# An FFT convolution whose last two tiles go through DRAM in more parts

## The chip, the cores and the metric

One core of one Trainium2 chip. The metric is device time in microseconds of one execution of the program; before the change it is 274.76 us, the median of three runs (272.75 to 276.08). Engines are named as in the profile: PE (TensorE matmuls), PEld (its weight loads), DVE (VectorE), ACT (ScalarE), POOL (GpSimd), SP (SyncE, which here only issues DMAs). ACTq and SPq are the DMA-issuing instructions of ACT and SP.

## The reference

```python
H = W = 224; C = 96; K = 7                      # x: (1, H, W, C) bf16, w: (K, K, C, C) bf16
wp = jnp.pad(w, ((0, H - K), (0, W - K), (0, 0), (0, 0)))
Xf = rfft2(x.astype(float32), axes=(1, 2))
Wf = rfft2(wp.astype(float32), axes=(0, 1))
Yf = einsum('bhwi,hwio->bhwo', Xf, Wf)
y = irfft2(Yf, s=(H, W), axes=(1, 2)).astype(bfloat16)
```

So y is the circular 7x7 convolution of a 224x224 image with 96 input and 96 output channels.

## The kernel before

The kernel computes the convolution in another way: a short Fourier transform along the height, the taps along the width. The height is cut into 8 blocks (j) of 28 output rows. Each block, with 6 rows of overlap, is transformed into 17 planes (s, real and imaginary part in r); for each plane the seven taps along the width are a chain of small matmuls over channels. The width is cut into 7 tiles (t = 0 to 6) of 32 pixels, handled as two phases of 16 positions (w). `TL` is the last tile, 6; the change speaks of tile 5 as the sixth.

Three kinds of work run for each tile:

- **A jobs** transform a tile's pixels. The pixels are loaded into two buffers, `xn_bufs` (118 partitions, 3072 elements, one for each half of the blocks), and PE writes the transform by way of PSUM into one of two `xf` buffers. Tile t+1's A jobs run in half-rounds 0 to 26 of tile t.
- **Rounds** (`b_round`): 17 a tile, one a plane. A plane is 33 matmuls of 96 columns (22 in the first and the last plane, `REAL`), with two PSUM banks, one scaling on ACT (tt_), two combining steps on DVE (u, v) and one sum (yf) on POOL or DVE. `yf` collects up to three planes (`YGRP`), then one DMA writes them to a scratch tensor in DRAM, `scr`, laid out [w][j][s][r, channel]. For the last tile these stores are issued by ACT, one round later (`puts`), and the very last one by SP.
- **C jobs** transform back. Planes come from DRAM with (j, s, r) on the partitions: three blocks make 102 rows. `load_t` loads them in five pieces a tile (`LT`: blocks 0-2 and 3-5, each in two halves of 8 positions, and blocks 6-7 in a special layout `tt2`) into `tt` tiles, which `pump` requests as buffers come free. The first request for tile t-1 is made by SP in round 3 of tile t (`queue_c`). A C job multiplies by the matrix `G` (102 x 84), two matmuls of 384 columns, casts from PSUM into a `yo` buffer (four of them, of which two are parts of a J buffer) and, each second job, stores to the output.

The order on each engine is the program's order. A round has two places for other work, `mid` (between its two banks) and `end`, called half-rounds k = 2s and 2s+1; `pace` spreads a list of jobs evenly from half-round a to b. `CQ` says how many C jobs of the two tiles before run in a tile: in tile 6, three of tile 4, then eleven of tile 5, the last of them due before half-round `k1` = 28.

The last tile's planes have no later tile beside which they could be transformed back. Its scratch is in three tensors, planes 0-8 (`scra`), 9-14 and 15-16 (`scrb`). The first is loaded by SP in round 11 into the free `xf` buffer (`tl_a`, 72 partitions for each half of the blocks); the others after the last round, by ACT (two DMAs) and SP (`tl_b`, 128 partitions). The matrices `GA` and `GB` (block-diagonal copies of parts of G, built by `g_parts` with small DMAs in tiles 3 and 4) hold four blocks at once. The last inverse is 16 chunks of 384 columns: `first` multiplies tl_a by GA into a PSUM bank, `second` adds tl_b times GB, `tail_evac` casts to bf16, alternating DVE and ACT. Eight `first` fill the eight PSUM banks; then `WARM` = 36 matmuls on a tile of zeros (`wu`) run; then come the 16 `second`. After each four chunks SP stores 336 KB to the output.

All instructions are recorded by a helper, so the profile gives line 87 for nearly everything; tiles tell them apart.

Of the kernel before, what the change touches and what calls it, by code (L numbers as in the profile page):

```python
# [8 lines left out]
BF16 = mybir.dt.bfloat16  # L9
# [5 lines left out]
B = 28  # L15
# [5 lines left out]
NJ = 8  # L21
# [12 lines left out]
YGRP = ((0, 3), (3, 6), (6, 9), (9, 12), (12, 15), (15, 17))  # L34
YGRPL = ((0, 3), (3, 6), (6, 9), (9, 12), (12, 15), (15, 17))
SA = 9
SB = 15
YMAX = 3
YBUF = 4
JGB = ((0, 3), (3, 6), (6, 9), (9, 12), (12, 15), (15, 17))  # L40
# [2 lines left out]
SH2 = (0, 8, 13, 17)  # L43
MERGE = ()
NP2 = 0
WARM = 36
BIAS = 3000.0


# [5 lines left out]
def kernel(  # L55
# [76 lines left out]
    def dma(out_ap, in_ap):  # L132
        return DE.dma_start(out=out_ap, in_=in_ap)
# [9 lines left out]
    KB = (NJ * 2 * (SB - SA), NJ * 2 * (NS - SB))  # L143
    assert sum(KB) == 128
    XW = 2 * TW * C
    xn_bufs = [cpool.tile([R, XW + 32], BF16, name=f"xn{i}") for i in range(2)]

# [341 lines left out]
    def b_round(t, s, mid, end, ydve=False, planes=()):  # L489
# [5 lines left out]
            1: (Jb[:, 6], Jb[:, 3], Jb[:, 2]),  # L495
            2: (Jb[:, 5], Jb[:, 1], Jb[:, 0]),
        }
        for (y0, y1) in (YGRPL if t == TL else YGRP):
# [77 lines left out]
            end()  # L576
        if s == y1 - 1:
            dst, yo0 = scr_tiles[t], 0
            if t == TL:
                i = (s >= SA) + (s >= SB)  # L580
                dst, yo0 = scr_tiles[(t, i)], (0, SA, SB)[i]
# [25 lines left out]

    TW2 = 2 * TW * C
    tl_all = xf_bufs[(TL + 1) % 2].rearrange("c p r s w j -> c (p r s w j)")
    tl_a = [tl_all[0:KA, g * TW2:(g + 1) * TW2].rearrange("p (w e) -> p w e", e=2 * C) for g in range(2)]  # L610
    tl_b = tl_all[:, 2 * TW2:3 * TW2].rearrange("p (w e) -> p w e", e=2 * C)

    def load_b(i, eng, nh):
        sb = scr_tiles[(TL, 1 + i)].rearrange("w j s (r e) -> (j s r) w e", r=2)
        for h in range(nh):
            w0, w1 = h * TW // nh, (h + 1) * TW // nh
            eng.dma_start(out=tl_b[i * KB[0]:i * KB[0] + KB[i], w0:w1], in_=sb[:, w0:w1])

    def g_parts():
        for j in range(4):  # L620
            dma(GA[j * 2 * SA:(j + 1) * 2 * SA, j * B:(j + 1) * B], G[0:2 * SA, 0:B])
            yield
        for j in range(NJ):
            for i, (s, s1) in enumerate(((SA, SB), (SB, NS))):
                n = 2 * (s1 - s)
                dma(GB[i * KB[0] + j * n:i * KB[0] + (j + 1) * n, j // 4, j % 4 * B:(j % 4 + 1) * B], G[2 * s:2 * s1, 0:B])
                yield

    yo_free = [J_bufs[2][0:4 * B, i * PXC * C:(i + 1) * PXC * C] for i in range(2)]
# [8 lines left out]
    def c_jobs(t):  # L638
        jobs = []
        w0 = t * 2 * TW  # L640
        for gi, h in LT:
            hold = {}
            nq = 2 if gi < 2 else 3

            def mk_(q, gi=gi, h=h, nq=nq, hold=hold):
                def put(j0, nj, px, npx, row, col):
                    dma(out[0, j0 * B:(j0 + nj) * B, w0 + px:w0 + px + npx, :].rearrange("h w c -> h (w c)"),
                        hold["yo"][row:row + nj * B, col:col + npx * C])

                def f():  # L650
                    if q % 2 == 0:
                        hold["yo"] = new_yo()
                    tt = tt_tiles[(t, gi, h)]
                    yo = hold["yo"]
                    nj = 2 if q == 2 else 3
                    for b in range(2):
                        pb = bank()[0:nj * B, 0:4 * C]
                        TE.matmul(pb, lhsT=G[0:nj * FR, 0:nj * B],
                                  rhs=tt[0:nj * FR, 4 * q + 2 * b:4 * q + 2 * b + 2, :].rearrange("p w e -> p (w e)"), start=True, stop=True)
# [10 lines left out]
                    if q == nq - 1:  # L670
# [79 lines left out]
    for r in range(NS + LAG):  # L750
# [18 lines left out]
        if r == PGRP[-2][1] + 1:  # L769
            assert not any(q[2] for q in qs[:len(PGRP) - 1])  # L770
            wtmp_cm.__exit__(None, None, None)
            t_pool = ctx.enter_context(tc.tile_pool(name="tt", bufs=NTT, side="right"))
            t2_pool = ctx.enter_context(tc.tile_pool(name="tt2", bufs=1, side="right"))
            yo_pool = ctx.enter_context(tc.tile_pool(name="yo", bufs=2, side="right"))
            g_pool = ctx.enter_context(tc.tile_pool(name="gp", bufs=1, side="right"))
            GA = g_pool.tile([KA, 4 * B], BF16, name="GA")
            GB = g_pool.tile([128, 2, 4 * B], BF16, name="GB")
            GE.memset(GA[:], 0.0)
            GE.memset(GB[:], 0.0)
        if r == NS + 3:  # L780
# [15 lines left out]
    cj = c_jobs(0)  # L796
    gp = g_parts()
    for t in range(2, NT):
        if t == TL:
            scr_tiles[t] = None  # L800
            scr_tiles[(t, 0)] = dr_pool.tile([TW, NJ, SA, 4 * C], BF16, name="scra")
            for i in range(2):
                scr_tiles[(t, 1 + i)] = dr_pool.tile([TW, NJ, (SB - SA, NS - SB)[i], 4 * C], BF16, name=f"scrb{i}")
# [40 lines left out]
    M4 = 4 * B  # L844

    def first(g, q):
        pc = bank()[0:M4, 0:4 * C]
        TE.matmul(pc, lhsT=GA[:], rhs=tl_a[g][:, 2 * q:2 * q + 2, :].rearrange("p w e -> p (w e)"), start=True, stop=False)
        return pc

    def second(g, q, pc, yo):
        TE.matmul(pc, lhsT=GB[:, g], rhs=tl_b[:, 2 * q:2 * q + 2, :].rearrange("p w e -> p (w e)"), start=False, stop=True)
        tail_evac(yo[0:M4, q % 4 * 4 * C:(q % 4 + 1) * 4 * C], pc, 4 * C)
    order = [(g, q) for h in range(2) for g in range(2) for q in range(4 * h, 4 * h + 4)]
    live = {k: first(*k) for k in order[:8]}
    for _ in range(WARM):
        TE.matmul(live[order[7]].rearrange("p (a b) -> p a b", a=3), lhsT=wu[:, 0:M4], rhs=wu[:].unsqueeze(1).to_broadcast([128, 3, 128]),
                  start=False, stop=False)
    LF = 4
    for i, (g, q) in enumerate(order):  # L860
        if q % 4 == 0:
# [40 lines left out]
```

## Time and profile before

| what | value |
|---|---|
| median of three runs | 274.76 us (272.75 to 276.08) |
| span of the profiled execution | 273.5 us |
| PE busy | 259.0 us (95%), 5149 matmuls |
| DVE, ACT, POOL busy | 213.0, 197.2, 94.8 us |
| DMA | 46.78 MB, mean 171 GB/s |
| PE matmul pb<-tt,Gm (C jobs) | 132, mean 326 ns |
| stores scr<-yf | 30 of 288 KB, 6 of 192 KB |
| loads tt<-scr | 24 of 336 KB, 6 of 288 KB, small ones |
| loads xf<-scra / xf<-scrb | 2 of 384 and 2 of 48 KB / 2 of 288 and 1 of 192 KB |

The profile is of one execution. Matmuls overlap, so their mean duration is longer than their spacing. A timeline line merges neighbouring instructions of a kind: start, duration, engine, operation, output<-input, count, and in brackets the idle time before it with what ended it. The chain of waits is followed back from the last instruction. The share called DMA is the mean busy share of the 16 DMA engines. DMA issues show when SP or ACT issued, not when data landed.

### The profile page before, as it was taken

The numbers are of one execution on the slowest core, as the hardware profiler recorded it, in microseconds if no ns is written. First come the engines' busy times: TensorE is split into PE (matmuls) and PEld (weight loads), VectorE is DVE, ScalarE is ACT, GpSimd is POOL, SyncE is SP. The second block draws the span as 40 slices with busy tenths as digits, with TensorE's granted clock in tenths as the row PEclk, the third lists the DMA queues.
The fourth block names the chain that finished last, engine by engine and source line by source line (L and its number), as shares of the span: only waits on it lengthen the run. The fifth ranks groups of instructions, "written<-read, shape, count | busy, mean of one in ns | idle before, by whom it ended". The sixth has DMA issues, their size and how long they took to land.

```text
span 273.5 us, 12147 instructions
## 1 busy us (share of the span) xinstructions
PE 259.0 (95%) x5149; PEld 237.7 (87%) x5149; DVE 213.0 (78%) x455; ACT 197.2 (72%) x485; POOL 94.8 (35%) x156
## 2 busy tenths in 40 slices
PE   8989998999999999999999999999999999899882
PEld 3659898999999989999999989999999999789661
DVE  5629799898979889779787887787977998788232
ACT  5529997668785657988988889888988865666022
POOL 7780032336446523431422222224144314224000
PEclk9999999999999999999999999999999999999999
DMA  6956110641112398996968487889678644797765
GB/s 177 222 119 169 52 47 2 168 135 48 46 47 88 105 288 149 274 263 166 310 172 248 116 228 217 200 205 313 253 194 181 204 162 132 154 297 195 196 120 180
DMA packets 46038, 46.78 MB, mean 171 GB/s; under 512 B 35150, under 2 KB 36954, under 8 KB 45886
## 3 DMA queue, kind: packets, MB, share of 16 engines
q1 hardware_dynamic: 43696, 43.94, 58.9%
q10 hardware_dynamic: 2288, 2.06, 2.7%
q8 instruction: 40, 0.66, 1.1%
q14 instruction: 14, 0.11, 0.1%
HBM read 24.65 MB, written 21.33 MB: 168 GB/s over the span
## 4 chain that ended last, share of the span: by engine, by line
PE 72%; DMA 11%; DVE 7%; ACT 5%; issue 2%; SPq 1%; POOL 1%; DVEq 0%; ACTq 0%
PE pb L87 72%; DMA wq<-in_w_dram 5%; ACT WF L87 3%; DVE WF L87 2%; DVE J L87 2%; DMA xf<-scrb 2%; DMA tt<-scr 2%; DMA scrb<-yf 1%; SPq L87 1%; DVE u L87 1%; DMA scr<-yf 1%; DVE v L87 1%; ACT xf L87 1%; DVE yf L87 1%; POOL yf L87 1%
## 5 line engine op out<-in xcount | busy, mean ns | idle before, releaser
L87 PE MATMUL pb<-WF,J 96*128 96x96 bf16 x2821 | 163.1, 206 | 1.1 <-DVE J L87 0.6
L87 PEld LDWEIGHTS <-J 96*128 96x128 bf16 x2821 | 138.2, 98 | 9.8 <-DVE u L87 1.5
L87 POOL TENSOR_TENSOR yf<-v,u 128x384 bf16<-128x384 f32 x79 | 77.8, 999 | 151.3 <-issue 88.0
L87 ACT CAST xf<-pb 96x408 bf16<-96x408 f32 (+3 forms) x143 | 67.3, 488 | 8.1 <-PE pb L87 6.3
L87 PE MATMUL pb<-WF,xf 96*128 96x96 bf16 x952 | 60.3, 206 | 1.1 <-ACT xf L87 0.5
L87 DVE TENSOR_TENSOR J<-xf 96x1824 bf16<-96x1824 bf16 (+1 forms) x84 | 57.6, 725 | 0.1
L87 PEld LDWEIGHTS <-xf 96*128 96x128 bf16 x952 | 47.3, 98 | 1.8 <-issue 0.9
L87 PE MATMUL pb<-Fm,xn 118*128 118x136 bf16 (+3 forms) x640 | 45.5, 199 | 0.9 <-DVE u L87 0.8
L87 ACT CAST WF<-pb 96x480 bf16<-96x480 f32 (+1 forms) x59 | 29.1, 573 | 6.8 <-PE pb L87 6.8
L87 PE MATMUL pb<-tt,Gm 102*84 102x384 bf16 (+1 forms) x132 | 32.4, 326 | 1.3 <-DMA tt<-scr 1.3
L87 ACT CAST J<-pb 84x384 bf16<-84x384 f32 (+1 forms) x65 | 28.0, 484 | 6.0 <-PE pb L87 3.0
L87 ACT CAST yo<-pb 84x384 bf16<-84x384 f32 (+1 forms) x66 | 28.2, 484 | 5.1 <-PE pb L87 5.1
L87 PEld LDWEIGHTS <-xn 118*128 118x128 bf16 x640 | 30.5, 97 | 1.2 <-issue 1.1
L87 DVE TENSOR_TENSOR J<-J 96x912 bf16<-96x912 bf16 (+2 forms) x42 | 22.8, 542 | 0.0
L87 PE MATMUL pb<-wq 98*128 98x120 bf16 (+1 forms) x288 | 21.3, 226 | 1.0 <-DMA wq<-in_w_dram 1.0
L87 PEld LDWEIGHTS <-wq 98*128 98x128 bf16 x288 | 19.4, 150 | 1.4 <-issue 1.4
L87 PE MATMUL pb<-wu 128*128 128x512 bf16 (+1 forms) x80 | 18.3, 392 | 1.0 <-DVE ct L87 1.0
L87 PEld LDWEIGHTS <-wu 128*128 128x128 bf16 (+1 forms) x80 | 9.4, 120 | 8.8 <-issue 3.3
L87 DVE TENSOR_TENSOR yf<-v,u 128x384 bf16<-128x384 f32 x26 | 14.7, 566 | 0.9
L87 DVE CAST WF<-pb 96x480 bf16<-96x480 f32 (+1 forms) x13 | 7.5, 610 | 6.8 <-PE pb L87 6.7
L87 PEld LDWEIGHTS <-Gm 102*84 102x84 bf16 (+1 forms) x132 | 11.0, 117 | 2.0 <-DMA tt<-scr 1.4
L87 ACT CAST tt<-pb 112x384 bf16<-112x384 f32 x8 | 3.6, 479 | 11.1 <-PE pb L87 11.0
(385 smaller groups left out, 239.7 us busy)
## 6 DMA issues: line engine op xcount, KB each, us to landing
scr<-yf SPq DMA_DIRECT2D x30, 288.0 KB
xn<-in_x_dram SPq DMA_DIRECT2D x12, 672.0 KB
tt<-scr SPq DMA_DIRECT2D x24, 336.0 KB
out_dram<-yo SPq DMA_DIRECT2D x12, 252.0 KB
out_dram<-J SPq DMA_DIRECT2D x12, 252.0 KB
tt<-scr SPq DMA_DIRECT2D x6, 288.0 KB
wq<-in_w_dram SPq DMA_DIRECT2D x1, 1719.0 KB
WF<-in_x_dram SPq DMA_DIRECT2D x2, 672.0 KB
```

What stands on the lines that cost most here:

```text
L87: r = fn(*a, **k)
```

## The change

Four things change; the arithmetic does not.

1. Tile 5's scratch is two tensors, planes 0-7 and 8-16 (`PART5`), with store groups that fit (`YGRP5`). Its blocks 0-5 go, whole rows of 16 positions at once, into the two pixel buffers: the first part in round 14 of tile 5, the second in round 3 of tile 6. Rows there are ordered (part, j, s, r), so a reordered copy of G, `G5`, is built. Blocks 6-7 still go into one `tt2` tile, first part requested in round 1 of tile 6, second in round 3.
2. Tile 6's scratch is five tensors (`LPART`). Their loads are issued by SP in rounds 8, 11 and 14 (`LOADS`); the fourth part is loaded by ACT and the fifth by SP after the last round. `g_parts` makes the matching smaller copies of G.
3. In tile 6 the C jobs end before half-round 24 instead of 28 (`k1`).
4. The last inverse runs in 12 chunks of 512 columns; its output is stored after two and after three chunks of each group of three (8 stores). `WARM` is 22.

```diff
-SB = 15
+LPART = ((0, 6), (6, 9), (9, 12), (12, 15), (15, 17))
+LROW = (0, 48, 0, 48, 96)
+LOADS = (8, 11, 14)
+SP5 = 8
+YGRP5 = ((0, 3), (3, 6), (6, 8), (8, 11), (11, 14), (14, 17))
...
-WARM = 36
+WARM = 22
...
+    def load_l(i, eng):
+        s0, s1 = LPART[i]
+        sv = scr_tiles[(TL, i)].rearrange("w j s (r e) -> (j s r) w e", r=2)
+        halves = [(tl_a[g], g, 2) for g in range(2)] if s0 < SA else [(tl_b, 0, 1)]
+        n = NJ * 2 * (s1 - s0) // len(halves)
+        for buf, g, _ in halves:
+            eng.dma_start(out=buf[LROW[i]:LROW[i] + n].rearrange("p (w e) -> p w e", w=TW), in_=sv[g * n:(g + 1) * n])
+
+    PART5 = ((0, SP5), (SP5, NS))
+
+    def load_5(i, gis):
+        s0, s1 = PART5[i]
+        n = 2 * (s1 - s0)
+        sv = scr_tiles[(TL - 1, i)].rearrange("w j s (r e) -> (j s r) w e", r=2)
+        for gi in gis:
+            if gi < 2:
+                m = -(-3 * n // 16) * 16
+                r0 = i * 6 * SP5
+                dma(xn_bufs[gi][r0:r0 + m, 0:XW].rearrange("p (w e) -> p w e", w=TW), sv[gi * 3 * n:gi * 3 * n + m])
+                continue
+            if i == 0:
+                tt_tiles[(TL - 1, 2, 0)] = t2_pool.tile([128, 12, 2 * C], BF16, name="tt2")
+            tt = tt_tiles[(TL - 1, 2, 0)]
+            for j in range(2):
+                a, b = 2 * s0 + j * FR, (6 + j) * n
+                dma(tt[a:a + n], sv[b:b + n, 0:12])
+                a = 2 * s0 + 2 * FR
+                dma(tt[a:a + n, 4 * j:4 * j + 4], sv[b:b + n, 12:16])
...
-        k1 = 2 * NS if t < TL else 2 * NS - 6
+        k1 = 2 * NS if t < TL else 2 * NS - 10
...
-            if s == 3:
+            if s == 3 and t < TL:
                 queue_c(t - 1)
-            if t in (3, 4):
+            if t == TL - 1 and s == 14:
+                load_5(0, (0, 1))
+            if t == TL and s == 1:
+                load_5(0, (2,))
+            if t == TL and s == 3:
+                load_5(1, (0, 1, 2))
+            if t in (3, 4, 5):
                 next(gp, None)
-            if t == TL and s == SA + 2:
-                sv = scr_tiles[(TL, 0)].rearrange("w j s (r e) -> (j s r) w e", r=2)
-                for g in range(2):
-                    for p0, p1 in ((0, 64), (64, KA)):
-                        dma(tl_a[g][p0:p1], sv[g * KA + p0:g * KA + p1])
+            if t == TL and s in LOADS:
+                load_l(LOADS.index(s), DE)
...
-    load_b(0, SE, 2)
-    load_b(1, DE, 1)
+    load_l(3, SE)
+    load_l(4, DE)
...
-        if q % 4 == 3:
-            w0 = TL * 2 * TW + q // 4 * PXC
-            dma(out[0, g * M4:(g + 1) * M4, w0:w0 + PXC, :].rearrange("h w c -> h (w c)"), yo[0:M4])
+        if q % NC:
+            a, b = ((0, 2 * CW), (2 * CW, 3 * CW))[q % NC - 1]
+            c0 = (TL * 2 * TW + q // NC * PXC) * C
+            dma(out[0, g * M4:(g + 1) * M4].rearrange("h w c -> h (w c)")[:, c0 + a:c0 + b], yo[0:M4, a:b])
```

`CW` is 512 and `NC` is 3. In the C jobs of tile 5, blocks 0-5 are read from the pixel buffers with G5 in place of G.

More of the change, by code (lines that the diff above doesn't have):

```diff
@@ L142 @@
     KA = 4 * 2 * SA
-    KB = (NJ * 2 * (SB - SA), NJ * 2 * (NS - SB))
-    assert sum(KB) == 128
+    assert NJ * 2 * (NS - SA) == 128
     XW = 2 * TW * C
@@ L497, in b_round @@
         }
-        for (y0, y1) in (YGRPL if t == TL else YGRP):
+        for (y0, y1) in (YGRPL if t == TL else YGRP5 if t == TL - 1 else YGRP):
             if s == y0:
@@ L578, in b_round @@
             dst, yo0 = scr_tiles[t], 0
-            if t == TL:
-                i = (s >= SA) + (s >= SB)
-                dst, yo0 = scr_tiles[(t, i)], (0, SA, SB)[i]
+            if t >= TL - 1:
+                lp = LPART if t == TL else PART5
+                i = next(i for i, (p0, p1) in enumerate(lp) if p0 <= s < p1)
+                dst, yo0 = scr_tiles[(t, i)], lp[i][0]
             def put(eng=DE):
@@ L609 @@
     tl_all = xf_bufs[(TL + 1) % 2].rearrange("c p r s w j -> c (p r s w j)")
[L610 to L617, printed above, removed]
@@ L619, in g_parts @@
-    def g_parts():
[L620 to L626, printed above, removed]
+    tl_a = [tl_all[0:KA, g * TW2:(g + 1) * TW2] for g in range(2)]
+    tl_b = tl_all[:, 2 * TW2:3 * TW2]
@@ new lines, in g_parts @@
+    def g_parts():
+        for i, (s0, s1) in enumerate(LPART):
+            n = 2 * (s1 - s0)
+            for j in range(4 if s0 < SA else NJ):
+                r0 = LROW[i] + j * n
+                o = GA[r0:r0 + n, j * B:(j + 1) * B] if s0 < SA else GB[r0:r0 + n, j // 4, j % 4 * B:(j % 4 + 1) * B]
+                dma(o, G[2 * s0:2 * s1, 0:B])
+                yield
+        for s0, s1 in PART5:
+            n = 2 * (s1 - s0)
+            for j in range(3):
+                r0 = 6 * s0 + j * n
+                dma(G5[r0:r0 + n, j * B:(j + 1) * B], G[2 * s0:2 * s1, 0:B])
@@ L652, in f @@
                         hold["yo"] = new_yo()
-                    tt = tt_tiles[(t, gi, h)]
+                    if t == TL - 1 and gi < 2:
+                        tt, g_ = xn_bufs[gi][:, h * 8 * 2 * C:(h + 1) * 8 * 2 * C].rearrange("p (w e) -> p w e", w=8), G5
+                    else:
+                        tt, g_ = tt_tiles[(t, gi, h)], G
                     yo = hold["yo"]
@@ L657, in f @@
                         pb = bank()[0:nj * B, 0:4 * C]
-                        TE.matmul(pb, lhsT=G[0:nj * FR, 0:nj * B],
+                        TE.matmul(pb, lhsT=g_[0:nj * FR, 0:nj * B],
                                   rhs=tt[0:nj * FR, 4 * q + 2 * b:4 * q + 2 * b + 2, :].rearrange("p w e -> p (w e)"), start=True, stop=True)
@@ L669, in f @@
                         put(6, 2, 16, 8, 0, 0)
-                    if q == nq - 1:
+                    if q == nq - 1 and t < TL - 1:
                         held[gi == 2] -= 1
@@ L777 @@
             GB = g_pool.tile([128, 2, 4 * B], BF16, name="GB")
+            G5 = g_pool.tile([3 * FR, 3 * B], BF16, name="G5")
+            GE.memset(G5[:], 0.0)
             GE.memset(GA[:], 0.0)
@@ L798 @@
     for t in range(2, NT):
-        if t == TL:
+        if t >= TL - 1:
             scr_tiles[t] = None
-            scr_tiles[(t, 0)] = dr_pool.tile([TW, NJ, SA, 4 * C], BF16, name="scra")
-            for i in range(2):
-                scr_tiles[(t, 1 + i)] = dr_pool.tile([TW, NJ, (SB - SA, NS - SB)[i], 4 * C], BF16, name=f"scrb{i}")
+            for i, (p0, p1) in enumerate(LPART if t == TL else PART5):
+                scr_tiles[(t, i)] = dr_pool.tile([TW, NJ, p1 - p0, 4 * C], BF16, name=f"scr{'ab'[p0 >= SA]}{i}" if t == TL else f"scr5{i}")
         else:
@@ L844 @@
     M4 = 4 * B
+    CW = 512
+    NC = TW2 // CW // 2
     def first(g, q):
-        pc = bank()[0:M4, 0:4 * C]
-        TE.matmul(pc, lhsT=GA[:], rhs=tl_a[g][:, 2 * q:2 * q + 2, :].rearrange("p w e -> p (w e)"), start=True, stop=False)
+        pc = bank()[0:M4]
+        TE.matmul(pc, lhsT=GA[:], rhs=tl_a[g][:, q * CW:(q + 1) * CW], start=True, stop=False)
         return pc
     def second(g, q, pc, yo):
-        TE.matmul(pc, lhsT=GB[:, g], rhs=tl_b[:, 2 * q:2 * q + 2, :].rearrange("p w e -> p (w e)"), start=False, stop=True)
-        tail_evac(yo[0:M4, q % 4 * 4 * C:(q % 4 + 1) * 4 * C], pc, 4 * C)
-    order = [(g, q) for h in range(2) for g in range(2) for q in range(4 * h, 4 * h + 4)]
+        TE.matmul(pc, lhsT=GB[:, g], rhs=tl_b[:, q * CW:(q + 1) * CW], start=False, stop=True)
+        tail_evac(yo[0:M4, q % NC * CW:(q % NC + 1) * CW], pc, CW)
+    order = [(g, q) for h in range(2) for g in range(2) for q in range(NC * h, NC * h + NC)]
     live = {k: first(*k) for k in order[:8]}
     for _ in range(WARM):
-        TE.matmul(live[order[7]].rearrange("p (a b) -> p a b", a=3), lhsT=wu[:, 0:M4], rhs=wu[:].unsqueeze(1).to_broadcast([128, 3, 128]),
-                  start=False, stop=False)
+        TE.matmul(live[order[7]][:, 0:384].rearrange("p (a b) -> p a b", a=3), lhsT=wu[:, 0:M4],
+                  rhs=wu[:].unsqueeze(1).to_broadcast([128, 3, 128]), start=False, stop=False)
     LF = 4
     for i, (g, q) in enumerate(order):
-        if q % 4 == 0:
+        if q % NC == 0:
             yo = t_pool.tile([128, TW // 2, 2 * C], BF16, name="tt").rearrange("p w e -> p (w e)")
```

## The prediction

> **What bounds the kernel now.** I read the page's busy table first: TensorE (PE) is busy 259.0 of 273.5 us, so a round costs what its matmuls cost, unless PE waits. I then asked for the busy time of the last tile's rounds and of what follows them:
>
> ```profile
> core 0: us, PE busy (x) PEld busy (x) DVE busy (x) ACT busy (x) POOL busy (x), PEclk, DMA share, GB/s
> 226.00:254.20 28.20, 26.93 (x545) 24.91 (x543) 24.14 (x53) 17.27 (x45) 9.62 (x10) 1.00 0.78 197
> 254.20:273.50 19.30, 11.55 (x68) 8.45 (x66) 5.07 (x10) 3.63 (x8) 0.00 (x0) 0.97 0.59 164
> ```
>
> In the rounds PE misses 1.27 us. In the 19.3 us after them no engine is a bound. The chain of waits (start, length, what) names both:
>
> ```profile
> 226.80 2.65 DMA scr<-yf
> ...
> 229.54 4.19 DMA tt<-scr
> ...
> 233.77 16.59 PE pb L87 x318
> ...
> 254.56 0.56 DVE yf L87
> 255.12 0.02 issue
> 255.13 4.05 DMA scrb<-yf
> ...
> 259.20 4.70 DMA xf<-scrb
> ```
>
> Two round trips through DRAM are on it: tile 5's last planes (226.80 to 233.72) and the last tile's last planes (255.13 to 263.90). The timeline shows PE's idle time at the first, and what stands behind the second:
>
> ```profile
> 233.77 0.52 PE L87 MATMUL pb<-tt,Gm 102*84 102x384 bf16 x2 [1.27 <-DMA tt<-scr]
> ...
> 256.66 6.01 PE L87 MATMUL pb<-wu 128*112 128x384 bf16 x36
> ...
> 264.30 4.47 DVE L87 CAST tt<-pb 112x384 bf16<-112x384 f32 x8 [9.19 <-PE pb L87]
> ...
> 265.39 3.76 SPq L87 DMA_DIRECT2D out_dram<-tt  x4
> ```
>
> The 36 matmuls on zeros only keep PE's clock up. From 264.30 DVE and ACT cast 16 chunks, and four output stores follow. The trace also records each transfer's semaphore updates; "landed" below is the last of them.
>
> **Part 1: tile 5's inverse.** Before, its first inverse pair stands at half-round 9 of tile 6 (end of round 4). PE gets there at 232.50 and waits 1.27 us. The change makes the earlier transfer smaller, but not the one that gates. The last store still leaves after round 16 of tile 5, now with three rounds (288 KB) instead of two (192 KB, 2.65 us). Uncontended 288 KB stores landed in 2.09 us (issued 223.37) and 2.46 us (218.48), so the store is 0.2 to 0.5 us quicker or no slower. The first second-part load is 384 KB against 336 KB before. The 336 KB took 4.19 us, and the next 336 KB landed 1.79 us after it, so 48 KB more is 48/336 x 1.79 = 0.26 us. In front of it lie four new small loads for the seventh and eighth blocks (192 KB, issued in round 1 of tile 6): at the same rate up to 1.0 us, of which I count 0.3, because they have two rounds' start. The landing moves by -0.3 + 0.26 + 0.3, about +0.2 us (-0.5 to +1.1).
>
> The end of the C jobs goes from half-round 28 to 24 (k1), so the first new pair moves up to half-round 8, in the middle of round 4. PE arrives there 14 matmuls earlier (14 x 41 ns, from 1.37 us for the 33 of a bare round, 250.43 to 251.79: 0.58 us), and that work is left for after the wait. The stall becomes 1.27 + 0.58 + 0.2, about 2 us, and the end of the rounds moves by 0.58 + 0.2 = +0.8; where the store is quick and the small loads cost nothing it is +0.1, at worst +1.7. I take +0.7. The second 384 KB lands about 2.1 us after the first (384/336 x 1.79) and is wanted at half-round 10, also 2.0 us on: 0 to 0.5 us more at the bad end, which the range holds. The blocks behind it have over two rounds.
>
> The first-part loads (576 KB in round 14 of tile 5) go where the DMA share is 0.2 to 0.5 (220 to 224 us) and into pixel buffers that PE last reads at 217.5: nothing. If that cover were gone, it would be the store at 226.80 that suffers, inside the bound above. On SP they stand ahead of three output stores from 221.11, a delay of two issues of 0.35 us, against four output buffers: nothing. The copies for GA, GB and G5 grow from 20 to 38, each under 1 KB; 18 issues of 0.33 us on SP in tiles 4 and 5, where PE is busy 35.69 of 36.00 us (160 to 196) and waits for no transfer: 0 to 0.3, taken as 0.
>
> **Part 2: the last tile's round trip.** From the last sum (255.11) to the landing (263.90) it is 8.79 us. The store of 192 KB took 4.05 us beside four loads of the first scratch (issued 247.55, the last landed at 255.86) and two 252 KB output stores (252.64, 253.48); the same size took 2.65 us at 226.80. In the change the first scratch is asked for in rounds 8 and 11, and the output stores are two rounds earlier; left beside the store are the 288 KB load of round 14 and the 288 KB store of rounds 12 to 14. I take 2.85 us. The last load of 192 KB took 4.70 us behind 576 KB on the ACT queue; now 288 KB stand there. The two 288 KB loads landed 1.62 us apart (261.55, 263.17), so 4.70 - 1.62 = 3.1 us. Sum 5.95 for 8.75: -2.8 us (-3.2 if the store takes 2.65 and the load 2.93, that is the 3.47 us of the first 288 KB less 96/288 x 1.62; -1.0 if both keep most of the present contention).
>
> The new waits are on SP: its loads of rounds 8, 11 and 14 wait for the stores two rounds before them. Before, SP waited 6.3 us in three such places (longest 3.3 us). Behind them stand output stores, whose four buffers each serve two jobs, some 10 us of slack: nothing, or +0.5 if a buffer is late. In rounds 12 to 16 no evacuations of C jobs are left for ACT; the chain has 0.75 us of them at 250.67, but PE itself ends at 254.16, 0.95 us before the last sum, so I credit 0.
>
> **Part 3: the last inverse.** Sixteen chunks of 384 become 12 of 512. DVE does 6 x 0.68 us (its 96x512 casts: 676 ns) = 4.1 for 8 x 0.56 = 4.47; ACT 6 x 0.61 = 3.6. That is -0.3. Four stores of 336 KB become four of 224 and four of 112 KB, 8 issues of 0.32 us on SP, which casts 0.69 us apart cover. The last store was issued at 268.83 and took 3.62; the last piece is now a third of it, issued right behind the other two thirds. An 84 KB output store took 1.67 us and a 336 KB one 2.71 with little beside it, so up to 1 us is there; half of it goes into the backlog: -0.5. Sum -0.8 (-1.4 to +0.2, the upper end if eight issues and shorter rows cost more).
>
> [...]
>
> **The sum.** +0.7 - 2.8 - 0.8 = -2.9 us against the profiled execution: a span of 270.6. The runs' median, 274.76, is 1.26 above that span; with the same distance it is 271.8 (rounded down from 271.86). The bounds of this case: +0.1 - 3.2 - 1.4 = -4.5 gives 270.3; +1.7 - 1.0 + 0.2 = +0.9 gives 275.7, and 273.0 if only one of the three goes wrong.
>
> **Rivals.** (a) *The gain is paid back at tile 5's inverse.* The first second-part load takes as long as the longest 336 KB loads of this trace (6.33 us issued 201.14, 6.17 issued 186.51), 2.1 us more than the 4.19, and the second one stalls PE again by 0.5. Part 1 is then +0.7 + 2.1 + 0.5 = +3.3, the whole -0.3 us: 274.5. For it: 984 KB leave SP at once behind that store. Against: before, 1.08 MB did, and the first landed in 4.19 us.
>
> (b) *Slower: the clock falls before the last inverse.* With 22 matmuls on zeros (22 x 167 ns = 3.7 us) after eight chunks of 512, (27 such matmuls took 5.99 us at 11.23, 222 ns each, so 1.8 us) PE is idle from 254.16 + 0.7 + 1.8 + 3.7 = 260.4. If the data come at 255.11 + 0.7 + 5.95 = 261.8, the gap is 1.4 us, near the present 1.27. This trace has the fall once, 4.1 us after the last matmul's end (268.2):
>
> ```profile
> 272.00:272.50 0.50, 0.00 (x0) 0.00 (x0) 0.00 (x0) 0.00 (x0) 0.00 (x0) 0.79 0.00 0
> 272.50:273.00 0.50, 0.00 (x0) 0.00 (x0) 0.00 (x0) 0.00 (x0) 0.00 (x0) 0.50 0.00 0
> ```
>
> So a gap of 1.27 us is safe, one of 4.1 is not. It decides only if part 2 gains nothing (data at 264.6, gap 4.2). Then 16 matmuls of 512 columns at 444 ns (222 ns at the granted clock of 0.50) are 7.1 us against casts of 4.1: +3.0. With +0.7 and part 3's +0.2: +3.9, so 278.7. [...]
>
> (c) *The loads do not come earlier.* The stores on ACT's queue land late (4.34 to 4.71 us at 249.07 and 253.31), the round-14 load is issued only at about 254, and the last round trip keeps its contention: part 2 is -1.0, the sum -1.1: 273.7.
>
> **Chances.** The forecast's case 0.64, (a) 0.12, (b) 0.08, (c) 0.16. A measurement of this kernel can tell about 1% (2.75 us) from no change. The forecast's centre lies just beyond that bound; more of its case lies on the far side (0.48 of the 0.64), because the store and load of part 2 and the output backlog are bounded by rows with more traffic than will be left. The remaining 0.16, (a) but for 0.05 that ends slower, and (c) lie within 1%, but for 0.03 of (c) that falls beyond: faster 0.51, same 0.36, slower 0.13. The range goes from 269.3, the case's bound less half the 2.01 us by which the lowest run before lies under the median, to 274.9, which holds (c) and the middle of (a) and leaves out (b) and the tails of (a) and of the forecast.
>
> **What would show it.** Right: PE's wait for the load of tile 5's planes in round 4 of tile 6 is about 2 us and its transfer goes to the pixel buffers; the last store takes under 3 us, the last load about 3; the warm matmuls end 1 to 2 us before the first chunk; the last cast group on DVE lasts about 4.1 us with six casts; the clock is 1.00 there. Wrong: a second wait of PE in rounds 5 to 7; a store above 4 us; PE waiting for a bank that an output buffer holds; a clock of 0.5 in the last matmuls.

## The result, and the profile after

The kernel with the change takes 284.19 us (median of four runs, 282.09 to 286.99); before, run beside it, takes 274.53. The ratio is 1.033 [1.026, 1.040]: slower. Ratios compare runs in the faster of two states alone, so that the one of 286.99 us is left out. The prediction, 271.8 (269.3 to 274.9) and probably faster, was wrong. The profiled execution, at 282.09 us the lowest of the four, has a span of 280.3 us for 273.5. These 6.8 us are what the profiles can explain; the medians differ by 9.7, and what the other executions lost beyond that was not traced.

The chain of waits after (start, length, what), for the same stretch as before:

```profile
233.68 5.60 issue
239.28 17.10 PE pb L91 x286
...
263.48 2.90 DMA scrb<-yf
266.40 3.89 DMA xf<-scrb
270.38 4.69 PE pb L91 x13
```

The last round trip is shorter, as forecast: from the end of the last sum (263.46) to the landing (270.29) it is 6.83 us for 8.79. But the last sum comes 8.35 us later than before. The timeline shows where (start, length, engine, operation, output<-input; in brackets the idle time before it):

```profile
222.49 1.08 SPq L91 DMA_DIRECT2D xn<-scr  x2
...
225.99 0.34 SPq L91 DMA_DIRECT2D scr<-yf  x1
...
232.80 0.34 SPq L91 DMA_DIRECT2D out_dram<-yo  x1
233.24 1.38 SPq L91 DMA_DIRECT2D xn<-scr  x2
...
239.28 0.84 PE L91 MATMUL pb<-xn,G 102*84 102x384 bf16 x2 [8.12 <-issue]
```

At the first C job of tile 5 PE is idle for 8.12 us where it was 1.27. Tile 5's last store goes out at 225.99 and lands at 230.67; the load that PE waits for goes out only at 233.24 and lands at 239.19. Its data were there at 230.67, but SP stood at the output store of 232.80. Its waits say for what (in all, times, longest):

```profile
SPq L91 <- DMA scra<-yf: 7.3, 2, 4.5
```

That is a store of the last tile, issued by ACT at 230.63, landed at 232.74, whose data the output store doesn't use. The transfers' records in this trace give the reason: both count on the same completion semaphore. All 229 transfers of this profile (223 by SP, 6 by ACT) count on eight semaphores in turn, 28 or 29 on each, ACT's store stands eight places ahead of SP's output store, and none of the 229 was issued before the last one on its semaphore had landed; this output store went out 0.06 us after that. The cases below are given with the landings in their own traces.

The view of busy time by stretches (from:to, length, PE busy, ..., the granted clock third from the end) shows a second loss:

```profile
229.57:232.98 3.41, 1.59 (x35) 1.42 (x32) 2.91 (x6) 1.52 (x4) 1.02 (x2) 1.00 0.31 104
232.98:236.39 3.41, 0.00 (x0) 0.00 (x0) 0.69 (x2) 0.00 (x0) 0.00 (x0) 0.50 0.62 159
236.39:239.81 3.42, 0.53 (x2) 0.37 (x3) 0.00 (x0) 0.00 (x0) 0.00 (x0) 0.50 1.24 178
239.81:243.22 3.41, 3.41 (x37) 3.01 (x36) 0.56 (x1) 1.70 (x4) 0.97 (x1) 0.50 0.53 116
...
267.12:270.53 3.41, 0.49 (x4) 0.18 (x2) 0.00 (x0) 0.00 (x0) 0.00 (x0) 1.00 0.65 143
270.53:273.94 3.41, 3.41 (x9) 1.74 (x8) 2.08 (x3) 1.63 (x3) 0.00 (x0) 0.50 0.31 94
```

TensorE's granted clock is 0.50 from 232.98 to 243.22, so that PE works 3.94 us at half speed after the data are there, and again in the last inverse (270.53 to 273.94). In this trace all its changes lie on one grid of 3.413 us: those at 232.98, 243.22, 270.53 and 273.94 are 3, 8 and 1 of these steps apart. From the landing of the last load to that of the last output store it is 9.0 us, for 8.55 before.

The two spans differ by 6.8 us: last sum +8.35, last round trip -1.96, last inverse +0.45.

### The profile page after: what moved, and what is told of

Same layout as the page of the kernel before. It is cut to its first block, busy times and chain, and to the rows that moved or that the text cites. A ratio compares the mean times of both kernels' runs of the same rounds, so it can differ in the third digit from the quotient of the medians.

```text
span 280.3 us, 12127 instructions
## 1 busy us (share of the span) xinstructions
PE 259.2 (92%) x5127; PEld 236.9 (85%) x5127; DVE 212.7 (76%) x453; ACT 197.0 (70%) x483; POOL 95.5 (34%) x157
## 4 chain that ended last, share of the span: by engine, by line
PE 75%; DMA 7%; DVE 6%; ACT 4%; issue 4%; SPq 1%; POOL 0%; DVEq 0%; ACTq 0%
PE pb L91 75%; DMA wq<-in_w_dram 5%; ACT WF L91 3%; DVE J L91 1%; DMA xf<-scrb 1%; DVE u L91 1%; DVE WF L91 1%; DVE v L91 1%; DMA scrb<-yf 1%; SPq L91 1%; ACT xf L91 1%; DVE yf L91 1%; POOL yf L91 0%; DVE tt L91 0%; DVEq L939 0%
## 5 line engine op out<-in xcount | busy, mean ns | idle before, releaser
L91 PE MATMUL pb<-tt,Gm 102*84 102x384 bf16 (+1 forms) x116 | 28.5, 326 | 0.0
L91 PE MATMUL pb<-wu 128*128 128x512 bf16 (+1 forms) x66 | 15.2, 390 | 1.1 <-DVE ct L91 1.1
L91 PEld LDWEIGHTS <-wu 128*128 128x128 bf16 (+1 forms) x66 | 7.4, 114 | 7.9 <-issue 2.1
L91 PE MATMUL pb<-xn,G 102*84 102x384 bf16 x16 | 4.6, 376 | 8.1 <-issue 8.1
L91 ACT COPY xf<-xf 96x816 bf16<-96x816 bf16 (+3 forms) x20 | 11.2, 622 | 0.0
```

The source lines that it names most:

```text
L91: r = fn(*a, **k)
```

## The experiments

Each ratio is against before on the same chip.

**Which half.** e1 is the change without the sixth tile's part (tile 5 loaded by `load_t` into tt as before). e2 is the sixth tile's part alone (the last tile in its three tensors, 16 chunks, `WARM` 36, `k1` 28).

```diff
# e1
-            if t == TL - 1 and s == 14: load_5(0, (0, 1))
-            if t == TL and s == 1: load_5(0, (2,))
-            if t == TL and s == 3: load_5(1, (0, 1, 2))
-            if s == 3 and t < TL:
+            if s == 3:
# e2
-LPART = ((0, 6), (6, 9), (9, 12), (12, 15), (15, 17))
+LPART = ((0, 9), (9, 15), (15, 17))
-LOADS = (8, 11, 14)
+LOADS = (11,)
```

> The change without its part on the sixth tile (one scratch tensor, loads by the old queue, matrix G), with everything on the last tile as changed. Theory A (the loss is the sixth tile's second-part load, which PE waits for in round 4 of the last tile, with the clock's fall behind it): PE waits about 2 us there instead of 8.1 (before 1.27, plus 0.6 for the earlier half-round 8), the clock stays at 1.00 in the rounds, and the last round trip keeps its gain of 2.0 us (6.81 against 8.79); time 272 to 274. Rival B (the loss is on the last tile's side: its waits in SP's queue and the shorter warm-up): 281 to 284, as the change.

> The sixth tile's part alone; on the last tile everything as before (three scratch tensors, 16 chunks, 36 warm matmuls, C jobs until half-round 28). Theory A: PE waits 7 to 8 us in round 4 of the last tile, the clock falls to 0.50 for some 7 to 10 us, time 281 to 284. Rival B: 274 to 276, with a wait like before's 1.27.

e2: 281.41 us, 1.024 [1.018, 1.029], with a wait of 6.94 us at the same place. So the sixth tile's part makes most of the loss. e1: 278.07 us, 1.010 [1.003, 1.018]: the rest doesn't gain either. The profile, of its 280.8 us execution, the longest of the four, shows two reasons; how far they hold for the other three isn't shown. Its first C job, 0.58 us earlier in the round, waits 1.78 us, and that is enough for the clock:

```profile
232.08:235.50 3.42, 1.64 (x35) 1.49 (x34) 3.02 (x6) 1.42 (x4) 0.98 (x2) 1.00 1.11 224
235.50:238.91 3.41, 3.41 (x34) 2.88 (x34) 1.13 (x3) 1.70 (x4) 0.97 (x1) 0.50 0.86 172
```

A stretch of 3.41 us in which PE is busy for 1.64 us ends with the fall; the next one, fully busy, runs at half speed. Before, whose grid follows from its one fall (272.29), the stretch that holds the whole wait of 1.27 us has PE busy for 2.15 us, and the clock stays:

```profile
231.33:234.75 3.42, 2.15 (x45) 1.90 (x43) 3.39 (x7) 1.75 (x5) 0.07 (x1) 1.00 1.23 244
```

The other reason is the last store. From its issue to the landing it is 6.0 us, the -2.8 of the forecast, but its sum was done at 259.36, so that from the sum it is 9.3 us, no gain on 8.8. The chain of waits shows what it waited for:

```profile
257.66 4.96 DMA scrb<-yf
...
262.69 3.24 DMA scrb<-yf
...
265.94 2.76 DMA xf<-scrb
```

The first is ACT's store of planes 12 to 14, landed at 262.62. The last store uses none of its data; both count on one semaphore.

**The shared semaphore at tile 5's load.** e5 asks for the load ahead of the output store, in round 1; e6 also puts its two large pieces first, so that they take other semaphores.

```diff
# e6 (e5: load_5(0, (2,)) and load_5(1, (0, 1, 2)) in round 1)
             if t == TL and s == 1:
+                load_5(1, (0, 1))
                 load_5(0, (2,))
-            if t == TL and s == 3:
-                load_5(1, (0, 1, 2))
+                load_5(1, (2,))
```

> The change with the second-part loads moved from round 3 to round 1, so that they stand ahead of the first output store in SP's queue; the first of them now is the DMA that shares its semaphore with the scratch store that ACT issues in round 3. Theory L (what held SP until 232.80 is the shared semaphore: its earlier user, ACT's store, landed at 232.74): the load is still issued only at about 232.8, 0.4 us earlier than 233.24; PE's wait 7 to 8 us; time 283 to 284. Rival Q (the output store itself held the queue, by its casts or buffers): the load is issued when the last scratch store has landed, about 230.7; PE's wait about 5.5 us, time about 281.

> As the run before, but the two large second-part loads stand ahead of the small first-part loads of blocks 6 and 7 as well, so neither shares a semaphore with ACT's store. Theory L: the first load is issued when the last scratch store has landed, about 230.7; PE's wait 5 to 6 us instead of 8.1; the clock still falls; time 280 to 282. Rival (the semaphore does nothing): as the run before it.

e5: 281.75 us, 1.027 [1.021, 1.032]. The load took over the shared semaphore and with it the hold: issued at 233.23, ACT's store having landed at 233.22. e6: 281.29 us, 1.026 [1.018, 1.034]. The load goes out at 231.30, right behind the landing of the last store (231.28):

```profile
231.30 1.39 SPq L91 DMA_DIRECT2D xn<-scr  x2
...
236.62 0.83 PE L91 MATMUL pb<-xn,G 102*84 102x384 bf16 x2 [5.33 <-DMA xn<-scr]
```

So the hold is real, and it is not the whole: the wait shrinks from 8.12 to 5.33 us, because the load itself takes 5.2. In time the hold isn't clear of noise: 1.027 with it (e5), 1.026 without (e6). One reason is where the clock's fall and rise lay, at 235.89 and 242.71:

```profile
232.48:235.89 3.41, 0.00 (x0) 0.00 (x0) 1.32 (x4) 0.00 (x0) 0.00 (x0) 1.00 0.98 178
235.89:239.30 3.41, 2.68 (x22) 2.12 (x23) 0.56 (x1) 1.22 (x3) 0.00 (x0) 0.50 1.14 144
239.30:242.71 3.41, 3.41 (x40) 3.12 (x39) 0.53 (x2) 1.64 (x5) 0.99 (x1) 0.50 0.40 114
```

PE works 2.68 + 3.41 = 6.09 us at half speed here, where the change does 3.94: so (6.09 - 3.94)/2 = 1.1 us of the shorter wait are lost again.

**What the clock costs.** e10 puts 34 matmuls on zeros ahead of tile 5's first C job; e9 only makes the row before the last inverse longer (`WARM` 40 for 22).

```diff
# e10
-        add(km, k1, cn[:nnew])
+        add(km, k1, ([lambda: warm(34)] if t == TL else []) + cn[:nnew])
```

> The change with 34 matmuls of 512 columns on zeros (7.5 us at full clock) put ahead of tile 5's first C job, so that PE is busy while it waits for the second-part load; they compute nothing that is used. The wait itself stays (its end is set by the load). Theory: the clock does not fall in the rounds, and the 10.24 us at 0.50 of the change, 3.9 of them with work in them, go: 2 us less than the change. Rival: the fall costs nothing since DVE or the loads set the pace there: no difference.

> The change with 40 warm matmuls instead of 22, nothing else. The wait and fall of the clock in the rounds stay as they are; the second fall (270.53 to 273.94) goes. From the landing of the last planes to the last output's landing 7.5 to 8 us instead of 9.0; time 1 to 1.5 us less than the change. If the fall of the clock there costs nothing, since the casts are the bound: no difference.

e10: 279.54 us, 1.015 [1.004, 1.026], with the data no earlier than in the change:

```profile
230.83 7.50 PE L91 MATMUL pb<-wu 128*128 128x512 bf16 x34
...
239.21 0.49 PE L91 MATMUL pb<-xn,G 102*84 102x384 bf16 x2 [0.28 <-issue]
```

Its clock is 1.0 up to the last output stores, in the last inverse too (mean of the execution 0.996, for the change's 0.976). With the wait filled with useless work the ratio is 1.8% lower (1.033 to 1.015, the intervals just apart). Of the 4.1 us between the two profiles 2.5 come before the last sum, as expected of the clock in the rounds, and 1.0 in the last inverse, whose clock also stays. e9 shows the second part alone: 281.50 us, 1.025 [1.018, 1.033]; the fall in the last inverse is gone (its 13 matmuls take 3.09 us for 4.69), and landing to last output takes 8.05 us for the change's 9.0. The intervals of e9 and e10 overlap.

**Two attempts that missed.** e7 is e1 with `WARM` 40 and tile 5's C jobs from half-round 11 to 26; e8 is e6 with `WARM` 40 and the C jobs from 16 to 30. Both were to let the data come first.

```diff
# e7 (e8: 16 and 2 * NS - 4)
-        k1 = 2 * NS if t < TL else 2 * NS - 10
+        k1 = 2 * NS if t < TL else 2 * NS - 8
-        km = k0 + -(-(k1 - k0) * nold // (nold + nnew))
+        km = k0 + -(-(k1 - k0) * nold // (nold + nnew)) if t < TL else 11
```

> The last tile's side alone, as in e1, with two numbers moved: tile 5's C jobs begin at half-round 11 instead of 8 (and end before 26), and 40 warm matmuls instead of 22. Theory A with the clock: PE's wait for tile 5's planes is gone (before 1.27, e1 1.78 us), the warm matmuls last until the data land, no fall of the clock, the last inverse takes 7.6 us from the landing to the last output instead of 8.85 in e1; last round trip about 6 us against 8.8; in all 4 to 5 us under before, 270 to 272. If the gain of the round trip is eaten by something else: 274 to 276.

> The change with e6's order of the loads, tile 5's C jobs from half-round 16 to 30 instead of 8 to 24, and 40 warm matmuls. Theory A (the loss is PE's wait and the clock's two falls, not the work or the traffic of the new loads): no wait above 0.5 us in the rounds, clock 1.00 until the data land, time 271 to 274. Rival (the new loads or the squeezed C jobs cost by themselves): 277 or more.

e7: 281.56 us, 1.024 [1.015, 1.033]; e8: 285.76 us, 1.039 [1.030, 1.047]. No wait is left at e7's first C job, but its last inverse now waits for the second load of scra. The chain:

```profile
253.06 3.86 DMA scrb<-yf
256.94 3.86 DMA xf<-scra
```

The load uses no data of that store; both count on one semaphore. In e8 a load of tile 5's blocks 6 and 7 went out at 239.12, when an ACT store (235.84) with its semaphore had landed (239.10), and PE waited 3.40 us at 245.49. Both last stores were held in the same way: in e7 the sum was done at 254.76 and the store went out at 261.57, in e8 at 261.72 and 268.88, each when a load by ACT on its semaphore had landed (261.51 and 268.82). In the change, e1, e5, e7 and e8 it was each time another pair of transfers that shared a semaphore.

**The last tile by itself.** e11 is e1 with the C jobs where they were before (`k1` = 28) and `WARM` 40. e13 is e1 with ten matmuls on zeros in the wait and `WARM` 40. e12 is before with the last inverse alone in 12 chunks and eight stores (`WARM` 30).

> The change without the sixth tile's part, with the C jobs again ending at half-round 28 as before, and 40 matmuls on zeros. Compared with e1 (278.07 us): the C jobs meet the load 0.58 us later in the round, so PE's wait is 1.2 us and not 1.78, the window of 3.41 us is over 60% busy and the clock stays 1.0 in the rounds (-1.7 us, of which 0.58 is the wait); the longer row of zeros keeps it in the last inverse too (-1.3 us). The theory (the clock falls were e1's loss) then gives 274 to 275, and 272.5 if the whole -2.8 of the round trip and -0.8 of the last inverse come out. Rival (the gain of the last tile isn't real: the earlier loads only move the contention to the output stores): 275 to 277 with no clock fall. A miss of another kind: the output stores, now two rounds later, shift the order of the shared semaphores, and a load or a store waits over 3 us for another queue's transfer: 278 or more.

> Before, with the last inverse alone in 12 chunks of 512 and eight output stores (30 matmuls on zeros for 36, so that the row with its wider first chunks ends at about the same time). The prediction's term: -0.8 us (-1.4 to +0.2), so about 274.4 where before is 275.2; the time from the landing of the last load to the landing of the last output store is 7.75 us for 8.55. Rival (the splitting of the stores costs as much as the smaller last piece brings): 0 to +0.5 us, 8.5 to 9 us. The clock at the second matmuls is 1.0 in both.

> e1 (278.07 us) with ten matmuls of 128x512 on zeros (2.2 us) ahead of tile 5's first C job and 40 in place of 22 ahead of the last inverse: PE isn't idle in the wait of 1.78 us, so the clock stays 1.0 in both places. The matmuls themselves end 0.4 us after the data. Theory: 278.07 - 1.6 (3.41 us at half speed, some 90% busy) + 0.4 - 1.3 = 275.5, less if e1's own profile was a bad one. Rival (the clock falls cost nothing beyond the waits): 278.

e12: 273.90 us, 0.9945 [0.991, 0.998]: this part of the change is a gain, and the only kernel here whose interval lies below 1. Landing to last output takes 8.06 us for 8.55 in its profile. e11: 279.60 us, 1.019 [1.013, 1.025]; e13: 278.51 us, 1.015 [1.009, 1.020]: misses. Neither clock fell in the rounds, PE had done them at 256.0 in e11, and still the data of the last planes landed at 268.23. The timeline of its DMA issues:

```profile
255.14 0.33 ACTq L91 DMA_DIRECT2D scrb<-yf  x1
258.82 0.34 SPq L91 DMA_DIRECT2D out_dram<-yo  x1
258.84 0.36 ACTq L91 DMA_DIRECT2D xf<-scrb  x1
259.21 0.37 SPq L91 DMA_DIRECT2D xf<-scrb  x1
259.67 0.54 SPq L91 DMA_DIRECT2D scrb<-yf  x1
265.36 0.32 SPq L91 DMA_DIRECT2D xf<-scrb  x1
```

The output store at 258.82 shares its semaphore with ACT's store of 255.14 (landed 258.76). The last store, whose sum was done at 256.95, stands behind it on SP and goes out at 259.67, together with two loads of 288 KB; it takes 5.67 us for the 2.90 of the change. In e13 the last store goes out at 260.02 in the same way and takes 5.75.

Four edits take hold of what stands ahead of that store. e14 is e11 with the last tile's stores by SP; e17 is e11 with them by POOL; e18 is e11 with the load of planes 9 to 11 by ACT after the last round; e16 is e12 with the stores by SP.

```diff
# e14, e16 (e17: put(GE))
-                puts.append(lambda: put(SE))
+                puts.append(lambda: put(DE))
```

> e11 (279.6 us) with the last tile's stores of rounds 2 to 14 issued by SP in place of ACT, so that no SP transfer shares a semaphore with a store of another queue. In e11 SP's loads of the last tile went out at 253.10 and 259.21 us right as an ACT store landed (250.91 to 253, 255.14 to 258.8), so that the last load but one of 288 KB ran beside the last store (5.67 us). Theory (the shared semaphores hold the loads back): these loads go out within 1 us of round 11 and round 14 of the tile, the last store takes under 3.5 us, from the last sum to the landing of the last load it is 6 to 7 us and not 8.6, and the time is 275 to 277 (-2 to -3 us and a clock that stays 1.0 in the last inverse, against SP's waits for the sums, 0 to +1). Rival (the DMA engines are the limit there): the store and load stay at 8 to 9 us and the time at 279.

> e12 (before with the last inverse in 12 chunks, 273.9 us) with the last tile's stores by SP. In the profile of before SP waits 6.3 us in three places for transfers of the first scratch, and PE's last wait ends at the load. If these waits hold the first scratch's loads (249.33, 6.44 us in e12, PE idle 1.84 us for them), it is 1 to 2 us faster: 272 to 273. Rival (SP in order behind the sums delays the output stores and loads): 274 to 276.

> e11 (279.6 us) with the last tile's stores of rounds 2 to 14 issued by POOL, which also makes the sums. In e11 the last store went out at 259.67, 0.5 us behind a load that SP could only issue when ACT's store (255.14) had landed, though PE had done its rounds at 256.0 already; in e14 SP, issuing all stores in order, sent it at 259.60 behind a load that waited for its own store. With the stores on a third queue nothing ahead of the last store waits for a store but the load of planes 9 to 11. Theory (what is queued on SP ahead of the last store eats the gain): the last store goes out within 1 us of its sum, at about 257, the data land 6 to 7 us later, and the time is 275 to 277. Rival (the transfers themselves are the limit): the store and load take 8 us or more, 278 to 279. POOL's own cost of issuing a transfer isn't known from these traces: if it holds the sums, they come 1 us or more late, and 278 to 280 follows for that reason.

> e11 (279.6 us) with the load of planes 9 to 11 issued by ACT after the last round in place of SP in round 14. SP then has only two output stores ahead of the last store. If one of them still shares a semaphore with ACT's store of planes 12 to 14, the last store goes out at 259 as in e11 and the time is 279 or more; if none does, it goes out at 257, and with 576 KB of loads now behind it as in before the round trip takes 8 to 9 us: 276 to 278.

e14: 279.02 us, 1.014 [1.007, 1.020], a miss: nothing is shared, but SP, which now issues all stores in order, holds the last one (259.60) behind a load that waits for its own store (254.68 to 258.59). e18: 278.19 us, 1.014 [1.004, 1.023]; the last store again goes out late, at 258.63, behind an output store held until 257.35 by a shared semaphore. e17: 273.21 us, 0.996 [0.992, 1.000], 2.3% below e11's ratio for one edit:

```profile
251.82 0.33 SPq L91 DMA_DIRECT2D xf<-scrb  x1
253.05 0.56 POOL L91 DMA_DIRECT2D scrb<-yf  x1 [0.96 <-DVE u L91]
254.46 0.35 SPq L91 DMA_DIRECT2D scrb<-yf  x1
257.87 0.34 ACTq L91 DMA_DIRECT2D xf<-scrb  x1
258.32 0.32 SPq L91 DMA_DIRECT2D xf<-scrb  x1
```

The last store goes out 1.0 us after PE's last round (253.49), and the span is 271.0 us. What SP had to issue ahead of the last store ate most of the gain in e11: from the last sum to the landing it is 7.7 us for 11.3, and of these 3.6 us 2.7 are the late issue, 0.9 the transfers' own time. (2.4 us of the difference between these two profiles are older: the row of 21 matmuls ahead of tile 5's first C job starts at 233.12 in e11 and at 230.72 in e17, before the first of the moved stores lands; what made it isn't shown. Its lowest run, 278.56 us, is 1.012 of that chip's before, e17's highest, 275.65, is 1.007.) e16: 274.32 us, 0.996 [0.992, 1.000]: no clear change from e12.

**Both again, with a third queue.** e15 is e9 with the stores by SP; e19 is the change with the stores by POOL and nothing else; e20 is e12 with them by POOL.

> The change with 40 matmuls on zeros (e9: 281.5 us) and the last tile's stores by SP. Theory: the first output store of the last tile no longer waits for ACT's store, and the sixth tile's second load goes out at about 231.3 us in place of 233.5, as in e6, where that took 1.3 us off PE's wait (7.4 to about 5.5 us; the load itself still takes 5 to 6 us), and the last tile's loads go out in their rounds: 278 to 280. Rival (no gain): 281.5.

> The change with one edit: the last tile's stores of rounds 2 to 14 by POOL in place of ACT. e17 against e11 showed 2.2% for the same edit. Here the first output store of the last tile no longer waits for ACT's store, so tile 5's second load goes out when the last store has landed (231.3 us in e6), PE's wait is 5.0 to 5.5 us and not 8.1, the clock falls for two windows in place of three (-1 us), and the last store goes out with its sum. Theory (the shared semaphores make the loss, but the sixth tile's load of 384 KB remains slower than the 336 KB one): 284.2 - 2.6 - 1 - 1 = 279 to 280, that is 1.5 to 2% slower than before. If the sixth tile's part costs nothing without the sharing: 273 to 275.

> e12 (12 chunks alone, ratio 0.9945) with the last tile's stores of rounds 2 to 14 by POOL. It tells how much of e17 (ratio 0.996) is the last tile's split into five parts: where the split brings its -2.8 us once no semaphore is shared, e20 is slower than e17 by 1 to 2 us (274 to 275); where the split brings nothing that the other queue doesn't, e20 equals or beats e17 (272 to 273).

e15: 281.92 us, 1.024 [1.018, 1.031], no change from e9 though the wait is 5.26 us for 7.43; e19: 281.88 us, 1.029 [1.023, 1.034]. In e19 no semaphore is shared with a store of another queue, and the wait is still there (the profile is of its longest run, 285.62 us):

```profile
240.21 0.84 PE L91 MATMUL pb<-xn,G 102*84 102x384 bf16 x2 [4.85 <-DMA xn<-scr]
```

Its last store took 4.40 us and its load 5.4. So the sixth tile's part loses by its own transfers. The shared semaphore lengthens the wait, but no pair of runs here (e5 and e6, e9 and e15, the change and e19) shows clear of noise that it costs time at this place. e20: 272.78 us, 0.997 [0.993, 1.000], like e17: the five parts bring nothing that can be told from zero over the 12 chunks alone. In its profile e17's round trip is 1.1 us shorter than e12's (7.7 for 8.8), which the times don't show; why stays open.

## Why the prediction was wrong, step by step

**Part 1, the sixth tile: the failed step.** The prediction took +0.7 us, at worst +1.7; measured to the last sum it is +8.35. Three terms of it and one that is missing failed. From the last store's issue to the landing of the load it was 6.92 us before (226.80 to 233.72) and is 13.20 (225.99 to 239.19):

| term | as predicted | measured |
|---|---|---|
| last store, 2.65 us before | 0.2 to 0.5 quicker, or no slower | 4.68: +2.03 |
| from its landing to the load's issue, 0.09 before | nothing for what SP is moved past | 2.57: +2.48 |
| first load, 4.19 us before | +0.26 for 48 KB, +0.3 for small loads | 5.95: +1.76 |
| half a round earlier | +0.58 | +0.58 in the wait |
| clock after the wait | not counted | 3.94 us at half speed: +1.97 |

With the 0.8 us by which the change was ahead until then, that makes 8.0 of the 8.35 us; 0.3 isn't assigned.

The first line: "The first-part loads (576 KB in round 14 of tile 5) go where the DMA share is 0.2 to 0.5 ...: nothing." They landed at 227.4 and 229.1, so the store, behind them on the same queue, ran beside them. The prediction named the price of this, the store at 226.80, and then kept it inside a bound drawn from stores without such neighbours. With those loads ahead it took 4.40 us (e19), 4.68 (the change), 5.15 (e6) and 5.26 (e15); without them the last store, of 192 KB, took 2.65 (before) and 2.89 (e14). The small loads behind it aren't the reason: e6 asks for them later, and the store took 5.15. But no run moved the first-part loads alone, so their part is argued and not shown.

The second line is shown by e5 and e6, as a wait and not as a time. The prediction read SP's order and the data each transfer needs. It missed what these traces show, that a transfer went out only when the last one on its semaphore had landed, also where another engine had issued that. The trace of before holds the records for it (203 transfers on eight semaphores, 25 or 26 on each): there a load of tile 5's planes goes out at 237.29, when ACT's store of 231.43, of another tile, had landed (237.23) on its semaphore.

The third line: the nearest row was not the 336 KB load of 8 x 112 rows, but the 384 KB one of 16 x 64 rows (xf<-scra, 5.02 us), which has the shape of the new load; how much of the 1.76 us is shape and how much traffic no run separates. Rival (a) carried this term (+2.1) and said 274.5; the other two lines were in no rival.

**The clock** was in rival (b), at the last inverse only, with "a gap of 1.27 us is safe, one of 4.1 is not". The runs put the point far lower: 1.78 us is not safe (e1). Stretches of the 3.413 us grid at full clock, with the time for which PE was busy in them, and the granted clock in the stretch after:

| stretch from | PE busy | clock after |
|---|---|---|
| before, 268.87 | 0 | 0.50 |
| e6, 232.48 | 0 | 0.50 |
| the change, 267.12 | 0.49 us (14%) | 0.50 |
| the change, 229.57 | 1.59 us (47%) | 0.50 |
| e1, 232.08 | 1.64 us (48%) | 0.50 |
| the change, 273.94 | 1.76 us (52%) | 1.00 |
| before, 231.33 | 2.15 us (63%) | 1.00 |

So a stretch needn't be idle for a fall to follow. The share isn't the whole of it either: on e1's grid a stretch of its setup ends at 20.46 us with 2.55 us (75%) busy, and the 32 matmuls at 21.02 take 1.91 us for 1.10 before; in before no fall follows the 2.46 us (72%) from 16.29. What decides there isn't shown.

**Part 2, the round trip.** Predicted -2.8: store 2.85, load 3.1. Measured 2.90 and 3.89, -1.96. With the whole change the gain came in part: from the last sum to the landing it is 6.3 to 7.2 us in the change, e6, e9 and e10, 7.9 in e5, 8.2 in e19 and 9.5 in e15, for 8.8 before. With the last tile's part alone it is 9.3 us in e1, 11.3 in e11, and 7.7 in e17, where nothing is held. That SP's waits for its loads in rounds 8 to 14 cost "nothing, or +0.5" is wrong for these: transfers ahead of it and shared semaphores hold the last store for 3.3 us in e1, 2.7 in e11, 2.4 in e13 and 5.1 in e18. One bound of the sum is off: with part 2 alone at its worst it gives 273.7, not 273.0.

**Part 3, the last inverse.** Predicted -0.8 (-1.4 to +0.2). In the change it is +0.45 because of the fallen clock; alone (e12) the ratio is worth -1.5 us [-2.5, -0.5]. The DVE casts measured 4.1 us as predicted (six of 690 ns). e12 can't separate the eight stores (112 and 224 KB) from the 12 chunks.

**Rivals.** (a) named the place and a third of the price. (c) isn't what the change did, whose last round trip gained 2.0 us, but e11 shows its mechanism. The blind spot was common to all: each worst case was bounded alone, and none followed a wait in the rounds into the clock.

## What to carry to other kernels

A stall had two prices here, its length and what the clock did after it (in the change 8.12 us, and 3.94 us of work at half speed): work out from the trace how busy PE is in each 3.41 us of the clock's grid. Useless matmuls in a wait that can't be avoided kept the clock up (e10: 34 of them in 7.50 us, mean clock 0.996). Before an urgent transfer is placed, look up in the trace which earlier transfer of any queue holds its semaphore, and what is queued ahead of it; transfers whose data were ready were held for 2 to 7 us by ones that they had nothing to do with (the change, e1, e7, e8). Measure a round trip from the end of the work that it waits for, not from its own issue. Price a load by a row of its own shape, beside the traffic that the edit itself adds.

## What the runs showed of the hardware

- In the change's trace the clock changed only on a grid of 3.413 us, and the phase decided the cost: a wait of 5.33 us (e6) left 6.09 us of work at half speed, one of 8.12 us (the change) 3.94.
- A 192 KB store took 2.9 us with one load of 288 KB and one store of 288 KB begun 1.7 to 2.4 us before it (the change), and 5.7 us beside two loads and an output store begun within 0.9 us of it (e11, e13).
- POOL issued a store in 0.56 to 0.82 us (e17) for ACT's 0.33, and its stores of 288 KB landed in 6.6 us (scra, median of three) and 4.0 us (scrb, median of two). Its last sum wasn't late by it: the last store went out 1.0 us after PE's last round, as before.
